# Turning reciprocal row sums on TensorE before their trip through memory, and taking sines two channel blocks at a time

## The chip, the core and the metric

One core of one Trainium2 chip runs the whole program. Its engines work side by side, each in its own order: TensorE (PE; its weight loads are PEld), VectorE (DVE), ScalarE (ACT), GpSimd (POOL) and SyncE (SP), which here issues every transfer between the chip's memory (DRAM) and the on-chip buffers. The metric is the time of one execution on the device in microseconds (us), as a median of runs.

## What is computed

Causal attention over 4 batches, 12 heads, 448 positions and 64 channels per head; a gated block on its result; and a mixing block with sines and cosines. All in float32, 768 channels wide. Cut to what matters:

```
scores = mask(q @ k.T / 8);  attn = exp(scores - max);  attn = attn / (sum(attn) + 1e-9)
x = attn @ v                                   # (batch, 448, 768)
gate = sigmoid(causal_conv5(x, conv_w));  x = (gate * (x @ w_val)) @ w_out
theta = x @ w_theta
y = w_tok_r @ (x * cos(theta)) + w_tok_i @ (x * sin(theta))
u = x + y
out = u + relu(u @ w_ch)
```

## The kernel before

Attention works on pairs of heads, `g` = 0 to 23, six pairs to a batch. `attn_iter(g)` is a generator of ten steps: it transposes the probabilities of pair `g - 1` (`attn_PT`), makes the scores of pair `g` in three portions (`attn_S`: matmuls, then a masked row maximum on DVE at L321, then the exponential with its row sum on ACT at L113), transposes q and k of pair `g + 1` (`attn_T`), and multiplies with v (`attn_AV`, L366).

The division by the row sums is put off: `attn_X1` (L426) multiplies the transposed result by a tile `rb` that holds the reciprocals, one per position, spread over the 64 channels of each head. The reciprocals come out with positions down the partitions (`rec`, 112 partitions by 8), and must be laid along the free axis. In the first batch (`g` < 6) `attn_W` does that with a widened copy and four TensorE transposes. From `g` = 6 on, 18 times, `attn_R` writes `rec` to a DRAM tile `rows` (L389), and `attn_B` reads each head's 448 values back, broadcast over 64 partitions (L415, two transfers). `attn_B` is kept behind the load of the next v.

Everything after the attention is `dense(b)`, a generator as well: six output blocks (`e`) each of x @ w_val, of @ w_out, of the mixing block and of @ w_ch. `gemm` (L496) makes one block: each 128x128 weight block and the activations are split into a high and a low part, and three products of 128x448 are summed, 18 matmuls for six blocks of the inner axis. In the first batch the weights arrive as 64-bit words that DVE and ACT make into floats (`to_f32`, L146 to L153) and POOL and DVE split (L102, L105, L108); the results are stored to DRAM (`plain`, `scratch`) for the later batches, which fetch them (L240, L244).

In the mixing block `theta(e)` copies the angles from the product (L551), reduces them to one turn on DVE (L552, L553), takes the absolute value, and takes a sine (L564) and a cosine (L565) on ACT, each times x (L566 on DVE, L567 on POOL or DVE). The angle tiles `z` rotate over three buffers, which the raw `tok` weights of the first batch use too (`load_tok`). `ztr(e)` transposes both halves on TensorE (L577, seven 128x128 blocks) and splits them (L582 on ACT, L108 on DVE); `tok(e)` (L591) is 21 matmuls with the token weights. Sine and the exponential live in different tables of ACT, so a sine after an exponential is preceded by an ACT_TABLE_LOAD, and the reverse.

A rate table (`RATE`) says after how many steps of `dense(b)` the next step of the attention of batch `b + 1` is written into the program. The order that each engine finally has is then made by a scheduler that replays the written order on a model of the chip: within an engine it may move an instruction ahead of one that waits. `tc.issue_after` pins some instructions: the sines behind the last two exponentials (`PIN`), `attn_B` behind the next v. A PSUM tile of the tags other than "mm" is one of six buffers that rotate.

Of the kernel before, what the change touches and what calls it, by code (L numbers as in the profile page):

```python
# [9 lines left out]
F32 = mybir.dt.float32  # L10
F32R = mybir.dt.float32r
I32 = mybir.dt.int32
# [35 lines left out]
def kernel(  # L48
# [110 lines left out]
    def load_tok(c):  # L159
        t = pool.tile([P, NZ * P], F32, tag=("zt_h", "zt_l")[c % 2], name="tok_raw")  # L160
        for a, w in enumerate((w_tok_r, w_tok_i)):
            r = pool.tile([P, S, 2], I32, tag="z", name="tok_bits", bufs=3)
            nc.sync.dma_start(
                out=r[:CP].rearrange("p n two -> p (n two)"), in_=w[c * CP : (c + 1) * CP, :]
            )
            to_f32(t[:CP, a * S : (a + 1) * S], r[:CP])
# [210 lines left out]
    def attn_R(g):  # L377
# [5 lines left out]
        if g < NP:  # L383
            wide = pool.tile([CP, NC, 2, D], F32, tag="m2k", name="wide", bufs=2)
            nc.vector.tensor_copy(wide, rec.rearrange("p h c -> p c h").unsqueeze(3).broadcast_to((CP, NC, 2, D)))
            wides[g] = wide
            return
        rows = dram.tile([2, NC, CP], F32, tag="rows", name="rows", bufs=2)
        nc.sync.dma_start(out=rows.rearrange("h c p -> p h c"), in_=rec)  # L389
        row_at[g] = rows  # L390
# [125 lines left out]
    def dense(b):  # L516
# [30 lines left out]
        def theta(e):  # L547
            pt = yield from gemm(x2_hl)
            z = pool.tile([P, 2, S], F32, tag="z", name="z", bufs=3)
            t, kk = z[:, 1, :], z[:, 0, :]  # L550
# [7 lines left out]
            else:  # L558
                nc.scalar.activation(kk, t, AF.Abs)
            zri[e] = z  # L560
            with ExitStack() as st:
                for ins in exps[-PIN:]:
                    st.enter_context(tc.issue_after(ins.ins))
                nc.scalar.activation(t, t, AF.Sin, scale=TWO_PI)  # L564
                nc.scalar.activation(kk, kk, AF.Sin, bias=halfpi, scale=-TWO_PI)  # L565
            nc.vector.tensor_tensor(out=kk, in0=kk, in1=x2f[e], op=ALU.mult)  # L566
            (nc.vector if Z_DVE[b] else nc.gpsimd).tensor_tensor(out=t, in0=t, in1=x2f[e], op=ALU.mult)  # L567
            yield

# [32 lines left out]
        yield from theta(1)  # L602
        for e in range(KC):
            if e + 2 < KC:
                g = theta(e + 2)
                next(g)
                yield
                ztr(e)
                yield from g
            elif e + 2 == KC:  # L610
                ztr(e)
                ztr(e + 1)
            yield from tok(e)

        def finish(e):
# [21 lines left out]
    def attn_iter(g):  # L637
# [9 lines left out]
        yield  # L647
        attn_B(h)
        attn_S(g, (2,))
        yield  # L650
        attn_PT(a, (2, 3))
        attn_PT(b, (2, 3))
        yield
        attn_S(g, (3,))
        if h in wides:
# [99 lines left out]
```

## Time and profile before

| | |
|---|---|
| median of 3 runs | 787.95 us (785.98 to 791.84) |
| the profiled execution | 786.97 us |
| its span, first to last instruction | 785.2 us |
| TensorE busy (PE / weight loads) | 727.4 us (93%) / 580.6 us (74%) |
| VectorE, ScalarE, GpSimd busy | 421.5, 403.8, 305.1 us |
| mean granted TensorE clock | 0.966 |
| SP's transfers | 123.86 MB in 148237 packets; 88175 of the program's packets are under 512 bytes |

All figures but the first row come from one profiled execution. An engine's busy time is the union of its instructions. A row of the trace gives the start and the length of an instruction or of a run of them, and in brackets how long its engine sat idle ahead of it and what ended that idle time. [...]

### The profile page before, as it was taken

To read this page: it belongs to the slowest core of one execution; us is meant where nothing else is said; L and a number is where in the kernel's file an instruction comes from. 1 tells how busy PE (TensorE), PEld (TensorE's weight loads), DVE (VectorE), ACT (ScalarE), POOL (GpSimd) and SP (SyncE) were. 2 spreads that over 40 slices of the span, in tenths; PEclk is the share of its full clock that TensorE was granted. 3 is DMA by queue.
4 is the path that set the end of the run, shared out by engine and by line. 5 is a ranking of instruction groups with operands and counts; after the bars stand their busy time and mean duration, and the time that the engine had idled before them with its cause. 6 is when DMAs were issued, how large, how long until landed. Compare 5 with 4: busy or idle time off the path is not lost.

```text
span 785.2 us, 11877 instructions
## 1 busy us (share of the span) xinstructions
PE 727.4 (93%) x3989; PEld 580.6 (74%) x3989; DVE 421.5 (54%) x1026; ACT 403.8 (51%) x975; POOL 305.1 (39%) x331
## 2 busy tenths in 40 slices
PE   6999786878989989999899999999899999999997
PEld 3665655755867777777677887887777788898996
DVE  5887596749646645354546644544547523115531
ACT  5877355648666543645867423434857512125401
POOL 1799725755547473755163400022051141201100
PEclk9999879888989999999999999999999999999999
DMA  9664369688734399989934297786424277774222
GB/s 233 158 192 116 88 193 142 202 181 276 131 117 115 76 225 216 321 228 218 249 85 58 72 202 157 231 205 122 169 73 45 73 184 202 202 218 140 82 73 80
DMA packets 148298, 124.62 MB, mean 159 GB/s; under 512 B 88175, under 2 KB 125837, under 8 KB 148237
## 3 DMA queue, kind: packets, MB, share of 16 engines
q1 hardware_dynamic: 148237, 123.86, 62.7%
q8 instruction: 32, 0.52, 0.3%
q14 instruction: 29, 0.24, 0.1%
HBM read 94.66 MB, written 29.16 MB: 158 GB/s over the span
## 4 chain that ended last, share of the span: by engine, by line
PE 50%; ACT 5%; DMA 4%; DVE 3%; POOL 2%; issue 2%; SPq 0%; ACTq 0%; POOLq 0%
PE ps_mm L496 29%; PE ps_mm L591 9%; PE ps_s L313 3%; PE ps_av L366 3%; PE ps_tr L343 3%; DMA cv_raw<-in_moe_w_ch_dram 2%; PE ps_tr L577 1%; DMA q_raw<-in_q_dram 1%; PE ps_tr L618 1%; ACT L564 1%; ACT prob L113 1%; PE ps_tr L291 1%; DMA scratch<-w_hl 1%; POOL w_hl L105 1%; POOL gate L454 1%
## 5 line engine op out<-in xcount | busy, mean ns | idle before, releaser
L496 PE MATMUL ps_mm<-act_hi,w_hl 128*128 128x448 f32 x864 | 276.6, 384 | 15.8 <-POOL w_hl L105 6.6
L496 PEld LDWEIGHTS ps_mm<-act_hi,w_hl 128*128 128x128 f32 x864 | 165.0, 193 | 45.6 <-issue 10.6
L496 PE MATMUL ps_mm<-act_lo,w_hl 128*128 128x448 f32 x432 | 160.0, 371 | 0.0
L113 ACT ACTIVATE prob<-ps_s,negm 112x112 f32<-112x112 f32 (+1 forms) x192 | 94.8, 500 | 57.6 <-DVE negm L321 34.9
L321 DVE CUSTOM_DVE_ANT_0 ps_s<-ps_s,mask 112x112 f32<-112x112 f32 (+1 forms) x192 | 84.4, 462 | 52.7 <-PE ps_s L313 51.2
L496 PE MATMUL ps_mm<-x_hi,w_hl 128*128 128x448 f32 x264 | 83.9, 388 | 6.2 <-POOL w_hl L102 2.6
L496 PEld LDWEIGHTS ps_mm<-act_lo,w_hl 128*128 128x128 f32 x432 | 83.8, 194 | 5.9 <-issue 0.7
L313 PE MATMUL ps_s<-kt,qt 64*112 64x112 f32 (+3 forms) x384 | 82.0, 447 | 4.0 <-ACT prob L113 2.2
L105 POOL TENSOR_TENSOR act_lo<-x2f,act_hi 128x448 fp32r<-128x448 f32 x36 | 41.7, 1157 | 110.3 <-DVE act_hi L508 72.2
L105 POOL TENSOR_TENSOR w_hl<-cv_raw,w_hl 128x384 fp32r<-128x384 f32 x62 | 64.3, 1039 | 24.1 <-ACT w_hl L224 22.6
L591 PE MATMUL ps_mm<-wtok_h,zt_h 128*128 128x448 f32 x168 | 65.2, 388 | 4.4 <-ACT zt_h L582 4.4
L343 PE MATMUL ps_tr<-ident,prob 112*112 112x112 f32 x480 | 63.0, 265 | 5.9 <-DVE cv_raw L153 4.5
L343 PEld LDWEIGHTS ps_tr<-ident,prob 112*112 112x112 f32 x480 | 50.9, 135 | 19.5 <-DVE cv_raw L153 5.0
L591 PE MATMUL ps_mm<-wtok_h,zt_l 128*128 128x448 f32 x168 | 62.8, 374 | 0.0
L105 POOL TENSOR_TENSOR x_lo<-xf,x_hi 128x448 fp32r<-128x448 f32 x23 | 29.1, 1267 | 86.5 <-ACT x_hi L431 59.0
L496 PEld LDWEIGHTS ps_mm<-x_hi,w_hl 128*128 128x128 f32 x264 | 51.6, 198 | 14.8 <-DVE hf L534 4.2
L591 PE MATMUL ps_mm<-wtok_l,zt_h 128*128 128x448 f32 x168 | 62.1, 370 | 0.0
L567 POOL TENSOR_TENSOR z<-z,x2f 128x448 f32<-128x448 f32 x18 | 20.7, 1153 | 105.2 <-ACT z L564 104.5
L356 ACT COPY pt<-ps_tr 112x448 f32<-112x448 f32 (+3 forms) x132 | 52.2, 431 | 14.0 <-PE ps_tr L343 13.9
L454 POOL TENSOR_TENSOR gate<-gate,tp 128x448 f32<-128x448 f32 x48 | 55.7, 1163 | 1.9
L366 PE MATMUL ps_av<-pt,v_raw 112*64 112x448 f32 (+3 forms) x384 | 55.2, 406 | 0.0
L313 PEld LDWEIGHTS ps_s<-kt,qt 64*112 64x112 f32 x384 | 32.1, 178 | 28.1 <-issue 14.0
(97 smaller groups left out, 1166.3 us busy)
## 6 DMA issues: line engine op xcount, KB each, us to landing
w_hl<-scratch SPq DMA_DIRECT2D x120, 384.0 KB, 4.1
scratch<-w_hl SPq DMA_DIRECT2D x48, 384.0 KB, 4.7
q_raw<-in_q_dram SPq DMA_DIRECT2D x48, 112.0 KB, 3.5
k_raw<-in_k_dram SPq DMA_DIRECT2D x48, 112.0 KB, 3.5
v_raw<-in_v_dram SPq DMA_DIRECT2D x24, 224.0 KB, 8.5
out_dram<-o SPq DMA_DIRECT2D x24, 224.0 KB, 3.5
cv_raw<-in_moe_w_val_dram SPq DMA_DIRECT2D x12, 384.0 KB, 5.0
plain<-cv_raw SPq DMA_DIRECT2D x24, 192.0 KB, 2.9
```

The lines of the kernel that those rows point to most:

```text
L105: nc.gpsimd.tensor_tensor(out=dst, in0=src, in1=f32(hi), op=ALU.subtract)
L113: exps.append(nc.scalar.activation(*args, **kw))
L291: nc.tensor.transpose(pt[:, c * CP : (c + 1) * CP], t[:, c, :, :].rearrange("p h d -> p (h d)"), ident[:CP, :CP])
L313: nc.tensor.matmul(at[j, c], lhsT=qt[j * D : (j + 1) * D, c * CP : (c + 1) * CP], rhs=kt[j * D : (j + 1) * D, :n], start=True, stop=True, ...
L321: ttr = nc.vector.tensor_tensor_reduce(out=at[j, c], in0=at[j, c], in1=mask[:, S - n : S], scale=-1.0 / math.sqrt(D), scalar=3.0e38, op0=A ...
L343: nc.tensor.transpose(pt[:CP, off : off + CP], prob[i, c][:, kc * CP : (kc + 1) * CP], ident[:CP, :CP])
L356: nc.scalar.copy(t, src)
L366: nc.tensor.matmul(av[g][j * D : (j + 1) * D, kc * CP : S], lhsT=tv[:, j, kc, :], rhs=pT.pop((2 * g + j, kc)), start=kc == 0, stop=kc == N ...
L454: nc.gpsimd.tensor_tensor(out=gt, in0=gt, in1=tp, op=ALU.add)
L496: nc.tensor.matmul(pt[:, :S], lhsT=a[:, kc % KH, :], rhs=x, start=kc == 0 and m == 0, stop=kc == KC - 1 and m == 2,)
L567: (nc.vector if Z_DVE[b] else nc.gpsimd).tensor_tensor(out=t, in0=t, in1=x2f[e], op=ALU.mult)
L591: nc.tensor.matmul(pt[:, :S], lhsT=a[:, m, :], rhs=w[:, m, :], start=m == 0 and n == 0, stop=m == NZ - 1 and n == 2,)
```

## The change

1. From `g` = 6 on, `attn_R` transposes `rec` on TensorE (112x8 to 8x112, into a PSUM tile of the six), copies it to a tile `rect` on DVE, and writes `rows` from that: 8 runs of 448 bytes in place of 896 runs of 4 bytes. 18 times each.
2. `attn_B(h)` stands later in `attn_iter`: ahead of the last portion of the scores, no longer ahead of the second.
3. The sines of blocks `e` and `e + 1` are written in one piece, `sines(e)`, at the end of the odd block's `theta`: sine, cosine, sine, cosine, then the four products.
4. The mixing loop is written in pairs: `theta(e + 2)`, `ztr(e)`, `theta(e + 3)`, `ztr(e + 1)`, `tok(e)`, `tok(e + 1)`. Before, the first half of `theta(e + 2)` stood ahead of `ztr(e)`, and `tok(e)` came straight after.
5. The angle tiles have four buffers in place of three.

```diff
     def load_tok(c):
...
-            r = pool.tile([P, S, 2], I32, tag="z", name="tok_bits", bufs=3)
+            r = pool.tile([P, S, 2], I32, tag="z", name="tok_bits", bufs=4)
...
+        pt = psum("tr")
+        nc.tensor.transpose(pt[: 2 * NC, :CP], rec.rearrange("p h c -> p (h c)"), ident[:CP, :CP])
+        rect = pool.tile([2 * NC, CP], F32, tag="rect", name="rect", bufs=1)
+        nc.vector.tensor_copy(rect, pt[: 2 * NC, :CP])
         rows = dram.tile([2, NC, CP], F32, tag="rows", name="rows", bufs=2)
-        nc.sync.dma_start(out=rows.rearrange("h c p -> p h c"), in_=rec)
+        nc.sync.dma_start(out=rows.rearrange("h c p -> (h c) p"), in_=rect)
...
-            z = pool.tile([P, 2, S], F32, tag="z", name="z", bufs=3)
+            z = pool.tile([P, 2, S], F32, tag="z", name="z", bufs=4)
...
             zri[e] = z
+            if e % 2:
+                sines(e - 1)
+            yield
+
+        def sines(e0):
             with ExitStack() as st:
                 for ins in exps[-PIN:]:
                     st.enter_context(tc.issue_after(ins.ins))
-                nc.scalar.activation(t, t, AF.Sin, scale=TWO_PI)
-                nc.scalar.activation(kk, kk, AF.Sin, bias=halfpi, scale=-TWO_PI)
-            nc.vector.tensor_tensor(out=kk, in0=kk, in1=x2f[e], op=ALU.mult)
-            (nc.vector if Z_DVE[b] else nc.gpsimd).tensor_tensor(out=t, in0=t, in1=x2f[e], op=ALU.mult)
-            yield
+                for e in (e0, e0 + 1):
+                    t, kk = zri[e][:, 1, :], zri[e][:, 0, :]
+                    nc.scalar.activation(t, t, AF.Sin, scale=TWO_PI)
+                    nc.scalar.activation(kk, kk, AF.Sin, bias=halfpi, scale=-TWO_PI)
+            for e in (e0, e0 + 1):
+                t, kk = zri[e][:, 1, :], zri[e][:, 0, :]
+                nc.vector.tensor_tensor(out=kk, in0=kk, in1=x2f[e], op=ALU.mult)
+                (nc.vector if Z_DVE[b] else nc.gpsimd).tensor_tensor(out=t, in0=t, in1=x2f[e], op=ALU.mult)
...
-        for e in range(KC):
-            if e + 2 < KC:
-                g = theta(e + 2)
-                next(g)
-                yield
-                ztr(e)
-                yield from g
-            elif e + 2 == KC:
-                ztr(e)
-                ztr(e + 1)
+        for e in range(0, KC - 2, 2):
+            yield from theta(e + 2)
+            ztr(e)
+            yield from theta(e + 3)
+            ztr(e + 1)
             yield from tok(e)
+            yield from tok(e + 1)
+        ztr(KC - 2)
+        ztr(KC - 1)
+        yield from tok(KC - 2)
+        yield from tok(KC - 1)
...
-        attn_B(h)
         attn_S(g, (2,))
         yield
         attn_PT(a, (2, 3))
         attn_PT(b, (2, 3))
         yield
+        attn_B(h)
         attn_S(g, (3,))
```

The program that the scheduler makes of it differs in far more places than these, since a moved step moves its neighbours. Three places matter below.

SP's queue around the trip of pair 8, in the first batch's dense part. Before, the write of `rows` stands ahead of a weight load, and the two reads of `rb` follow three transfers later:

```order
93 L389 DMA rows<-rec 112x8x1
94 L192 DMA cv_raw<-in_moe_w_theta_dram 128x3x256
95 L232 DMA scratch<-w_hl 128x768
96 L280 DMA v_raw<-in_v_dram 112x8x64
97 L415 DMA rb<-rows 64x448 x2
98 L232 DMA scratch<-w_hl 128x768
99 L192 DMA cv_raw<-in_moe_w_theta_dram 128x3x256 x2
```

In the changed program, at the same trip:

```order
93 L192 DMA cv_raw<-in_moe_w_theta_dram 128x3x256 x2
94 L393 DMA rows<-rect 8x112
95 L280 DMA v_raw<-in_v_dram 112x8x64
96 L232 DMA scratch<-w_hl 128x768 x2
97 L192 DMA cv_raw<-in_moe_w_theta_dram 128x3x256
98 L419 DMA rb<-rows 64x448
99 L232 DMA scratch<-w_hl 128x768
100 L419 DMA rb<-rows 64x448
101 L192 DMA cv_raw<-in_moe_w_theta_dram 128x3x256
```

The weight load now goes ahead of the write of `rows`, and the reads of `rb` still stand a few transfers behind it, with loads queued after them.

TensorE at the same pair. Before, the products with v (`ps_av`) stand behind 18 matmuls of a `gemm` that follow the transposes of k, of which the last rows are:

```order
278 L496 MATMUL ps_mm<-act_hi,w_hl 128x448 x2
279 L496 MATMUL ps_mm<-act_lo,w_hl 128x448
280 L496 MATMUL ps_mm<-act_hi,w_hl 128x448 x2
281 L496 MATMUL ps_mm<-act_lo,w_hl 128x448
282 L366 MATMUL ps_av<-pt,v_raw 64x448 x2
```

In the changed program the new transpose (`ps_tr<-ident,rec`) stands there, ahead of the products with v; from the transposes of k to it there are 20 matmuls of a `gemm`, of which the last rows are:

```order
296 L500 MATMUL ps_mm<-act_lo,w_hl 128x448
297 L500 MATMUL ps_mm<-act_hi,w_hl 128x448 x2
298 L500 MATMUL ps_mm<-act_lo,w_hl 128x448
299 L500 MATMUL ps_mm<-act_hi,w_hl 128x448
300 L389 MATMUL ps_tr<-ident,rec 8x112
301 L366 MATMUL ps_av<-pt,v_raw 64x448 x2
```

The products with v stand two matmuls later than before, and behind the transpose of `rec`.

ACT in the mixing block of the second batch. Before, every block's sine and cosine (`z<-z`, and `z<-z,halfpi`) have a table load ahead of them, and the exponentials (`prob`) another:

```order
453 L564 ACT_TABLE_LOAD
454 L564 ACTIVATE z<-z 128x448
455 L565 ACTIVATE z<-z,halfpi 128x448
456 L113 ACT_TABLE_LOAD
457 L113 ACTIVATE prob,sums<-ps_s,negm 112x112
```

In the changed program blocks 4 and 5 have theirs together:

```order
460 L113 ACTIVATE prob,sums<-ps_s,negm 112x448 x2
461 L575 ACT_TABLE_LOAD
462 L575 ACTIVATE z<-z 128x448
463 L576 ACTIVATE z<-z,halfpi 128x448
464 L575 ACTIVATE z<-z 128x448
465 L576 ACTIVATE z<-z,halfpi 128x448
```

Blocks 0 and 1 of the first three batches are still taken one by one there, with exponentials between them. Over the whole program the table loads go from 38 to 26.

## Rows read from the trace of the kernel before

**Rows 1.** Busy time by stretch: length, each engine's busy us, clock, DMA share, GB/s.
```profile
84.00:174.00 90.00, 71.43 (x351) 55.81 (x351) 64.06 (x148) 48.05 (x118) 47.29 (x55) 0.84 0.69 162
174.00:252.00 78.00, 70.71 (x348) 55.41 (x349) 53.37 (x119) 57.60 (x121) 42.66 (x47) 0.88 0.61 163
...
420.00:550.00 130.00, 130.00 (x753) 105.62 (x752) 68.43 (x167) 54.56 (x140) 28.38 (x26) 1.00 0.71 155
...
sum 785.20, PE 727.35 PEld 580.58 DVE 421.47 ACT 403.83 POOL 305.09; mean PE 80.82 PEld 64.51 DVE 46.83 ACT 44.87 POOL 33.90
```
**Rows 2.** TensorE in order of time: idle ahead of an instruction, and what ended it.
```profile
137.67 1.11 PE L496 MATMUL ps_mm<-act_hi,w_hl 128*128 128x448 f32 x2 [5.74 <-POOL w_hl L105]
...
174.14 1.12 PE L496 MATMUL ps_mm<-act_hi,w_hl 128*128 128x448 f32 x2 [5.78 <-ACT act_hi L510]
...
285.62 0.50 PE L343 MATMUL ps_tr<-ident,prob 112*112 112x112 f32 x3 [2.75 <-DVE cv_raw L153]
...
350.29 0.47 PE L496 MATMUL ps_mm<-act_hi,w_hl 128*128 128x448 f32 x1 [1.06 <-ACT w_hl L224]
...
376.50 0.47 PE L496 MATMUL ps_mm<-act_hi,w_hl 128*128 128x448 f32 x1 [1.52 <-DMA w_hl<-scratch]
```
**Rows 3.** The line that writes the reciprocals: count, issue time, time to landing.
```profile
L389 SPq DMA_DIRECT2D rows<-rec x18: 312/431/1304, 77.4 to 628.2; - x18
...
DMA to landing us min/median/max: 6.7/8.2/11.2
```
**Rows 4.** What SP's queue waited for: us in total, times, longest.
```profile
SPq L415 <- DMA rows<-rec: 68.4, 13, 7.5
```
**Rows 5.** Busy time, columns as in the first group, behind one such write (160.71).
```profile
161.00:169.00 8.00, 7.36 (x43) 6.46 (x39) 2.71 (x6) 3.40 (x7) 5.69 (x6) 1.00 0.64 57
```
**Rows 6.** Weight loads, us to landing: those issued in 161 to 169, then all.
```profile
cv_raw<-in_moe_w_theta_dram SPq DMA_DIRECT2D x1, 384.0 KB, 10.9
...
cv_raw<-in_moe_w_theta_dram SPq DMA_DIRECT2D x12, 384.0 KB, 5.5
```
**Rows 7.** The tile that the reciprocals are read back to: time to landing of its transfers.
```profile
DMA to landing us min/median/max: 2.7/3.9/7.3
```
**Rows 8.** Busy time, columns as in the first group, where the clock was low.
```profile
135.00:142.00 7.00, 3.98 (x13) 3.35 (x13) 2.36 (x7) 1.25 (x3) 5.85 (x7) 0.57 0.77 234
...
172.00:179.00 7.00, 4.86 (x16) 4.04 (x18) 4.39 (x10) 4.42 (x9) 4.88 (x6) 0.53 1.07 348
193.00:199.00 6.00, 5.03 (x16) 4.20 (x15) 5.20 (x12) 5.95 (x12) 1.79 (x2) 0.50 0.33 100
```
**Rows 9.** Groups of instructions: table loads, busy us and mean ns.
```profile
L564 ACT ACT_TABLE_LOAD x19 | 24.4, 1283 | 0.3
L113 ACT ACT_TABLE_LOAD x18 | 23.1, 1283 | 0.3
```
**Rows 10.** ACT in order of time, around one table load.
```profile
218.58 1.28 ACT L564 ACT_TABLE_LOAD   x1
219.88 0.58 ACT L564 ACTIVATE z<-z 128x448 f32<-128x448 f32 x1
```
**Rows 11.** TensorE in order of time in the mixing blocks: idle and what ended it.
```profile
190.61 0.98 PE L577 MATMUL ps_tr<-ident,z 128*128 128x128 f32 x7 [2.29 <-DVE z L566]
...
222.91 1.76 PE L577 MATMUL ps_tr<-ident,z 128*128 128x128 f32 x7 [1.93 <-ACT prob L113]
...
564.21 0.74 PE L591 MATMUL ps_mm<-wtok_h,zt_h 128*128 128x448 f32 x1 [1.46 <-ACT zt_h L582]
...
713.38 0.95 PE L577 MATMUL ps_tr<-ident,z 128*128 128x128 f32 x7 [1.22 <-DVE z L566]
```
**Rows 12.** The chain that ended last: start, us, what; one unbroken run of matmuls.
```profile
664.14 21.50 PE ps_mm L496 x106
```
**Rows 13.** Pair 10 in order of time: products with v, and the reciprocal.
```profile
239.02 1.25 PE L366 MATMUL ps_av<-pt,v_raw 112*64 112x448 f32 x6
...
241.53 0.19 DVE L382 RECIPROCAL rec<-rec 112x8 f32<-112x8 f32 x1
```

## The prediction

> **What bounds the kernel now.** I read the busy times by stretch first [rows 1]. TensorE is busy for 727.35 of 785.20 us, and from 420 to 550 us for every microsecond: there no other engine can give anything back. What can be won lies in the 58 us in which TensorE is idle, and in the stretches where its clock was at half. Both cluster in the first batch's dense part: from 84 to 174 us it is busy 71.43 of 90 us at a mean granted clock of 0.84, from 174 to 252 us 70.71 of 78 at 0.88. So the second view is TensorE in order of time, with what ended each idle stretch.
>
> The longest stops are 5.74 and 5.78 us [rows 2]. They end with POOL and ACT, but those had been idle too. Each stop lies some 13 us behind the issue of a write of reciprocals (the second write at 160.71). The third view is that line: 18 writes, which land 6.7 to 11.2 us after issue, median 8.2, for 3.5 KB each [rows 3]. SP, which cannot issue the read of `rb` before that, stood still for 68.4 us in 13 waits with all that is queued behind [rows 4]. And it is more than a wait: from 161 to 169 us the DMA engines are busy for 0.64 of the time and move 57 GB/s [rows 5], where they move 162 on average over 84 to 174 [rows 1]. The one weight load issued in that stretch, right behind the write, landed after 10.9 us, where the median of that line is 5.5 [rows 6]. The 896 runs of 4 bytes lie ahead of it on the same queue. So two things hold the weights: the queue in front of the engines, and the issuer.
>
> **Part A, the trip through memory.** Removed: 888 of 896 runs, 18 times. A write of 8 runs is not in this trace. Its landing is bounded from below by the fastest transfer of the same trip, 2.7 us for the reads back, and from above by their slowest, 7.3 (median 3.9) [rows 7]; I take 3, near the lower end, since the write is 32 times smaller than a read (3.5 against 112 KB). The load behind it then lands in some 5.5 us, 5.4 earlier, and that is nearly all of a 5.78 us stop. Five stops lie behind such a write, with a late load, store or fetch at their root: 5.74, 5.78, 2.75, 1.06 and 1.52, together 16.85 us [rows 2]. Behind the two long ones TensorE went on at half clock: 3.98 us busy at 0.57 and 4.86 us at 0.53 [rows 8], which lost 3.98 x 0.43 + 4.86 x 0.47 = 4.0 us. Upper bound 20.8. Not all of it comes back. DVE is busy 64.06 of the 90 us [rows 1]; without the two stops (11.5) and the slow clock (4.0) the same work would have to fit in 74.5 us, 86% of them, and the next wait for DVE is close. I take 0.6 of the bound, 13 us; the lower bound is half of the two long stops, 6.
>
> `attn_B`, moved later in the text, moves little: SP's queue still has the reads a few transfers behind the write. The pair's result is multiplied by `rb` a whole attention step later, so this I cost at nothing, under the cover of that step (some 30 us per pair in the dense part); without it, DVE would wait one read, 3.9 us.
>
> **Part B, the sines.** Removed are 12 table loads, 4 in each of the first three batches: 19 + 18 become 13 + 12, at 1.283 us each 15.4 us of ACT [rows 9]. ACT has room (57.60 of 78 us even from 174 to 252), so only what TensorE waits for counts. In the mixing blocks I find eleven idle stretches of TensorE that end with ACT, or with what hangs on a sine: four shown, 6.9 us [rows 11], and seven more of 0.61 to 1.41, 5.7 together. Behind three of them the clock was low: one shown, 5.03 us busy at 0.50, lost 2.5 us [rows 8]; the other two 2.7 and 1.3. Upper bound 12.6 + 6.5 = 19.1. The scheduler left blocks 0 and 1 of the first three batches one by one, so the stop of 2.29 us and its slow clock, at block 0 of the first batch, may stay. I take half of what follows in the first batch (idle 3.9 and clock 2.7: 3.3), most of 1.41 in the second and of 0.69 + 1.46 + 1.3 in the third (3, since nine more matmuls of a `gemm` now stand between the first transposes and the first `tok`), and in the last batch 1 of 1.22 + 0.69, since a whole block, 18 x 0.203 = 3.7 us [rows 12], now runs ahead of the first transpose. Together 7. Lower bound 0.
>
> ACT shows a table load at 218.58 with no idle time ahead of it, and the sine 0.02 us after its end [rows 10]: a switch costs the load alone. [...]
>
> **Part C, what it adds.** 18 transposes on TensorE. A matmul in an unbroken run takes 0.203 us for 448 columns [rows 12]; this one has 112, so 3.7 us is the upper bound for 18, and I take 3. 18 copies on DVE, by the reciprocal's 0.19 [rows 13] 3.4 us over the whole run, between work that DVE has slack for; with no slack (first batch, three of them) under 1. An additional PSUM tile of the six per pair is held from the transpose to that copy: free if the copy follows at once; up to the length of the waits below if not.
>
> And a new wait: TensorE now needs `rec`, in order, ahead of the products with v, and those are queued behind it. At pair 10 the products began at 239.02 and the reciprocal ended at 241.72 [rows 13]: had the transpose stood there, TensorE would have waited 2.7 us. Counted so, 12 of the 18 pairs would wait, 15.7 us in all. The scheduler put the transpose later, mostly behind a whole `gemm` block. Bounds 0 and 15.7; I take 4, nearer to the lower end, since outside the first batch and the mixing blocks the reciprocal was ready before the products began, or within a microsecond.
>
> **Sum.** 786.97 (the profiled execution; 1 us under the median of 787.95) - 13 - 7 + 3 + 4 = 774.
>
> **Rivals.** *DVE takes over.* Where the loads come earlier, DVE, at 86%, is late instead: waits keep their place and change their name. A 6, B 2, C 7: 786. For it: DVE's share in the first batch. Against: in the long stops DVE itself was idle.
>
> *The write stays slow.* Its time could be the queue ahead of it, not its runs. Then A is 0, B and C cancel: 787. Against: none of the 18 landed under 6.7 us, while a read 32 times as large does in 2.7.
>
> *Everything comes back.* A 20.8, B 19.1, C 3: 750. Against: the loads of blocks 0 and 1 remain, and DVE's share.
>
> *The transpose holds SP.* The write now waits for TensorE and for DVE's copy, and weight loads queue behind it on SP; TensorE reaches the transpose only through matmuls that need weights. If the block on SP merely moves from behind the write to ahead of it, A is 0 and the full 15.7 + 3.7 are paid: 787 + 19.4 - 7 = 799. It decides once the wait at the transpose is over 1 us on average over the 18 pairs. [...] Against: the queue listing has the weight loads mostly ahead of the write.
>
> **How the numbers follow.** Forecast 0.58 (its own range 764 to 781), everything back 0.10, DVE takes over 0.20, slow write 0.04, transpose holds SP 0.08. About 1% (8 us) is what a measurement of this kernel can tell from no change. Faster: 0.56 of the forecast and the 0.10, 0.66. Same: the rest of the forecast, 0.20 and 0.04, 0.26. Slower 0.08. The range leaves out the lowest half of "everything back" and what lies above the DVE case: 757 to 788.
>
> **What would show it.** A right: the write of `rows` lands in about 3 us, SP's wait for it falls from 68 to under 25 us, no TensorE stop over 3 us from 84 to 174, clock there above 0.92. B right: 25 loads of the two lines, fewer stops that end with ACT from 200 us on. C: idle ahead of the new transpose 4 us in all. I am wrong if the stops of the first batch remain at the same length with DVE or the transpose named, or if the write still lands after 6 us.

## The result

| | before | after |
|---|---|---|
| median | 789.89 us (785.98 to 793.18, 4 runs) | 752.54 us (749.83 to 753.45, 4 runs) |
| ratio to before, 95% interval | | 0.9523 (0.9468 to 0.9579) |
| the profiled execution, its span | 786.97, 785.2 us | 753.18, 751.3 us |
| TensorE busy | 727.4 us | 713.9 us |
| mean granted TensorE clock | 0.966 | 0.982 |

The change is worth 35 us or so, and lies 4.5 us under the range of the prediction (757 to 788, with 774 as the likeliest). TensorE's idle time in the span fell from 57.8 to 37.4 us, 20.4 less; its busy time fell by 13.5, although 18 transposes came in. Most of that is the clock. The granted clock is the share of its full speed that TensorE was given; busy time times the missing share is 727.4 x 0.034 = 24.7 us before and 713.9 x 0.018 = 12.9 after, an estimate from the mean clocks.

The first view of the profile after is TensorE by line: busy us and mean ns, then the idle time just ahead of the line's instructions, and what ended it. The first row is the `gemm`, the second and third are `tok` and `ztr` of the mixing block, the last is the new transpose of the reciprocals:

```profile
L500 PE MATMUL ps_mm<-act_hi,w_hl 128*128 128x448 f32 x864 | 267.2, 374 | 2.4 <-DVE w_hl L108 1.7 <-ACT act_hi L514 0.7
...
L603 PE MATMUL ps_mm<-wtok_h,zt_h 128*128 128x448 f32 x168 | 63.9, 380 | 0.0
...
L589 PE MATMUL ps_tr<-ident,z 128*128 128x128 f32 x168 | 23.5, 282 | 1.6 <-DVE z L579 1.6
...
L389 PE MATMUL ps_tr<-ident,rec 112*8 112x112 f32 x18 | 4.6, 258 | 7.9 <-ACT z L563 4.9 <-DVE rec L382 2.9
```

The kernel before, the same lines:

```profile
L496 PE MATMUL ps_mm<-act_hi,w_hl 128*128 128x448 f32 x864 | 276.6, 384 | 15.8 <-POOL w_hl L105 6.6 <-ACT act_hi L510 6.4 <-DMA w_hl<-scratch 1.5
...
L591 PE MATMUL ps_mm<-wtok_h,zt_h 128*128 128x448 f32 x168 | 65.2, 388 | 4.4 <-ACT zt_h L582 4.4
...
L577 PE MATMUL ps_tr<-ident,z 128*128 128x128 f32 x168 | 24.6, 281 | 6.8 <-DVE z L566 4.2 <-ACT prob L113 1.9 <-DVE xf L426 0.7
```

So two places were cleared. Ahead of the `gemm`, which waited for weights and their splits, 15.8 us became 2.4. In the mixing block 4.4 + 6.8 became 0.0 + 1.6. One place is new, the transposes, with 7.9 us.

By stretch, with the columns of [rows 1] (length, busy us of PE, PEld, DVE, ACT and POOL, clock, DMA share, GB/s):

```profile
84.00:174.00 90.00, 82.91 (x431) 64.49 (x431) 80.77 (x182) 60.80 (x146) 61.55 (x70) 0.94 0.70 206
174.00:252.00 78.00, 74.27 (x425) 59.58 (x426) 56.98 (x131) 53.84 (x125) 47.24 (x52) 0.98 0.51 153
```

In the first batch TensorE is busy for 82.91 of the same 90 us, where it was for 71.43 [rows 1], at a clock of 0.94 for 0.84. DVE did more there as well, 80.77 us, or 90% of the stretch: a share of 86% was not yet a bound.

SP's queue after, what it waited for: in total, times, longest.

```profile
SPq L393 <- DVE rect L391: 15.3, 10, 5.8
SPq L419 <- DMA rows<-rect: 8.1, 10, 3.1
```

The second row answers to [rows 4]: 68.4 us became 8.1. The first is the write waiting for its copy. Before, it waited for the reciprocal in its place, so SP is not held longer there:

```profile
SPq L389 <- DVE rec L382: 18.5, 6, 8.5
```

TensorE in order of time after: what is left of the longer stops, from the start of the dense part on.

```profile
109.20 1.18 PE L343 MATMUL ps_tr<-ident,prob 112*112 112x112 f32 x5 [2.98 <-DVE cv_raw L153]
...
171.64 0.68 PE L500 MATMUL ps_mm<-act_hi,w_hl 128*128 128x448 f32 x2 [1.71 <-DVE w_hl L108]
...
181.25 1.01 PE L291 MATMUL ps_tr<-ident,q_raw 112*128 112x112 f32 x4 [2.66 <-ACT prob L113]
...
360.65 0.26 PE L389 MATMUL ps_tr<-ident,rec 112*8 112x112 f32 x1 [2.67 <-ACT z L563]
...
537.95 0.26 PE L389 MATMUL ps_tr<-ident,rec 112*8 112x112 f32 x1 [2.24 <-ACT z L563]
...
686.17 0.95 PE L589 MATMUL ps_tr<-ident,z 128*128 128x128 f32 x7 [1.61 <-DVE z L579]
```

The stops of 5.74 and 5.78 us [rows 2] have no successor of their size.

### The profile page after: what moved, and what is told of

It is laid out like the page before. It is cut to its first block, busy times and chain, and to the rows that moved or that the text cites. A ratio compares the mean times of both kernels' runs of the same rounds, so it can differ in the third digit from the quotient of the medians.

```text
span 751.3 us, 11926 instructions
## 1 busy us (share of the span) xinstructions
PE 713.9 (95%) x4007; PEld 573.8 (76%) x4007; DVE 432.3 (58%) x1044; ACT 388.3 (52%) x963; POOL 307.6 (41%) x331
## 4 chain that ended last, share of the span: by engine, by line
PE 78%; DVE 10%; ACT 7%; issue 2%; DMA 1%; SPq 1%; POOL 0%; DVEq 0%; ACTq 0%
PE ps_mm L500 38%; PE ps_mm L603 13%; PE ps_s L313 8%; PE ps_av L366 6%; PE ps_tr L343 5%; ACT prob L113 2%; PE ps_tr L589 2%; PE ps_tr L291 2%; DVE ps_cv L146 1%; PE ps_tr L630 1%; DVE ps_cv L149 1%; DVE ps_s L321 1%; PE ps_mm L479 1%; ACT L575 1%; ACT L113 1%
## 5 line engine op out<-in xcount | busy, mean ns | idle before, releaser
L500 PE MATMUL ps_mm<-act_hi,w_hl 128*128 128x448 f32 x864 | 267.2, 374 | 2.4 <-DVE w_hl L108 1.7
L500 PEld LDWEIGHTS ps_mm<-act_hi,w_hl 128*128 128x128 f32 x864 | 161.0, 188 | 30.7 <-issue 15.7
L500 PE MATMUL ps_mm<-act_lo,w_hl 128*128 128x448 f32 x432 | 156.5, 364 | 0.0
L313 PE MATMUL ps_s<-kt,qt 64*112 64x112 f32 (+3 forms) x384 | 83.8, 443 | 5.2 <-ACT prob L113 1.7
L500 PEld LDWEIGHTS ps_mm<-act_lo,w_hl 128*128 128x128 f32 x432 | 81.3, 188 | 5.5 <-issue 0.8
L500 PE MATMUL ps_mm<-x_hi,w_hl 128*128 128x448 f32 x264 | 82.3, 381 | 1.4 <-DVE hf L538 1.0
L105 POOL TENSOR_TENSOR w_hl<-cv_raw,w_hl 128x384 fp32r<-128x384 f32 x62 | 64.5, 1043 | 15.8 <-ACT w_hl L224 14.2
```

The source lines that it names most:

```text
L105: nc.gpsimd.tensor_tensor(out=dst, in0=src, in1=f32(hi), op=ALU.subtract)
L313: nc.tensor.matmul(at[j, c], lhsT=qt[j * D : (j + 1) * D, c * CP : (c + 1) * CP], rhs=kt[j * D : (j + 1) * D, :n], start=True, stop=True, ...
L500: nc.tensor.matmul(pt[:, :S], lhsT=a[:, kc % KH, :], rhs=x, start=kc == 0 and m == 0, stop=kc == KC - 1 and m == 2,)
```

## The experiments

Two questions had to be told apart: which of the five parts of the change gave the time, and by what. The medians of before in these comparisons lie between 785.6 and 787.3 us; each kernel's ratio is to the runs of before beside it. The changed kernel's own ratio, 0.9523, is to a before of 789.89 us. So its distance to another kernel comes out 3 to 6 us larger by ratios than by medians; the text gives the medians' difference, the smaller of the two.

**Part 1 alone.** The reciprocals transposed, everything else as before.

```diff
+        pt = psum("tr")
+        nc.tensor.transpose(pt[: 2 * NC, :CP], rec.rearrange("p h c -> p (h c)"), ident[:CP, :CP])
+        rect = pool.tile([2 * NC, CP], F32, tag="rect", name="rect", bufs=1)
+        nc.vector.tensor_copy(rect, pt[: 2 * NC, :CP])
...
-        nc.sync.dma_start(out=rows.rearrange("h c p -> p h c"), in_=rec)
+        nc.sync.dma_start(out=rows.rearrange("h c p -> (h c) p"), in_=rect)
```

> The kernel before with part 1 of the change alone: the reciprocals transposed on TensorE and written as 8 runs of 448 bytes; attn_B, sines, mixing loop and three angle buffers as before. Theory 'the trip': the write of 896 runs held SP and the DMA queue, and both long stops of the first batch hang on it; five stops (16.9 us) and 4 us of slow clock go, 4 to 8 us are paid at the transpose: 768 to 775, no stop over 3 us from 84 to 174, SP waits under 20 us for rows. Rival 'the sines': the dense part's stops come from ACT and DVE being late, so the trip alone gives less than 8 us: 780 to 788, and stops of like length stay with another name. Rival 'only together': the scheduler's new order is what helps, and neither half gives more than a third of the 34 us.

Measured: 776.71 us, ratio 0.9887 (0.9845 to 0.9929), 9 us faster, and 1.7 us outside the range that the theory of the trip gave. The dense part is repaired as that theory says: no stop of TensorE from 84 to 174 us is over 2.4 us, and SP waits 9.2 us for `rows`. Its stretch, and the same two lines of the mixing block as above:

```profile
84.00:174.00 90.00, 81.21 (x420) 62.75 (x420) 77.21 (x181) 58.19 (x142) 60.28 (x70) 0.94 0.71 205
```

```profile
L595 PE MATMUL ps_mm<-wtok_h,zt_h 128*128 128x448 f32 x168 | 65.7, 391 | 7.8 <-ACT zt_h L586 7.8
...
L581 PE MATMUL ps_tr<-ident,z 128*128 128x128 f32 x168 | 24.1, 279 | 6.3 <-DVE z L570 4.6 <-ACT pt L356 0.9 <-DVE xf L430 0.8
```

From 84 to 174 us nearly all of the change is there already (81.21 busy, clock 0.94). But the stops of the mixing block, 11.2 us before, are now 14.1: part of what the trip gave seems to be lost at the next place.

**Parts 3 to 5 alone.** Sines, loop and buffers as in the change, with the old write and the reads in their old place.

```diff
-            z = pool.tile([P, 2, S], F32, tag="z", name="z", bufs=3)
+            z = pool.tile([P, 2, S], F32, tag="z", name="z", bufs=4)
...
+            if e % 2:
+                sines(e - 1)
...
+        for e in range(0, KC - 2, 2):
+            yield from theta(e + 2)
+            ztr(e)
+            yield from theta(e + 3)
+            ztr(e + 1)
```

> The kernel before with parts 3 to 5 alone: the sines of two blocks together, the mixing loop in pairs, four angle buffers; the write of 896 runs of 4 bytes and the place of attn_B as before. Theory 'the trip': the stops of 5.74 and 5.78 us stay, 8 to 13 us come back, all from the mixing blocks: 775 to 780. Rival 'the sines': 755 to 765, and the long stops of the first batch are gone though the write lands after 7 us or more. 26 table loads in either case.

Measured: 762.99 us, ratio 0.9711 (0.9678 to 0.9744), 23 us faster: the larger part of the change is here, in the range of the rival and not of the theory of the trip. One long stop stays; where the other was, the longest is of 2.07 us, though the write still lands 6.6 to 11.2 us after its issue:

```profile
135.89 1.01 PE L174 MATMUL ps_tr<-ident,tok_raw 112*128 112x112 f32 x4 [5.81 <-DVE cv_raw L153]
...
168.39 0.68 PE L496 MATMUL ps_mm<-act_hi,w_hl 128*128 128x448 f32 x2 [2.07 <-ACT act_hi L510]
```

The same two lines of the mixing block:

```profile
L599 PE MATMUL ps_mm<-wtok_h,zt_h 128*128 128x448 f32 x168 | 64.0, 381 | 2.4 <-ACT zt_h L590 2.2
...
L585 PE MATMUL ps_tr<-ident,z 128*128 128x128 f32 x168 | 22.5, 275 | 1.6 <-DVE z L575 1.6
```

**Part 1 undone in the changed kernel.**

```diff
-        nc.sync.dma_start(out=rows.rearrange("h c p -> (h c) p"), in_=rect)
+        nc.sync.dma_start(out=rows.rearrange("h c p -> p h c"), in_=rec)
```

> The changed kernel with part 1 undone: rec is written from its 112 partitions in 896 runs of 4 bytes, without the transpose and the copy; all else as changed. Theory 'the trip': 770 to 780, stops of 4 to 6 us some 13 us behind the first writes, the write lands after 7 us or more. Rival 'the sines': within 5 us of 752, since the write was only a symptom. The waits ahead of the transpose, 7.9 us in the changed kernel, are gone in either case.

Measured: 763.57 us, ratio 0.9711 (0.9677 to 0.9745), the same as parts 3 to 5 alone. Both forecasts missed: the time lies between their ranges, and the stops of 4 to 6 us did not come back (the longest behind the first two such writes are of 2.68 and 2.30 us), though the write lands after 6.5 us or more. The trip is worth 11 us in the changed kernel, 9 in the one before.

**Part 2 alone.** Only SP's queue changes its order.

```diff
-        attn_B(h)
         attn_S(g, (2,))
...
+        attn_B(h)
         attn_S(g, (3,))
```

> The kernel before with part 2 alone: the reads of rb are issued later; no other engine's order changes, only that of SP's queue. All theories: SP stands still for less than 68 us at the reads, since the write has more time to land ahead of them; if the issuer's standing still is what made the weights late, 5 us or more come back (780 or less); if it is the 896 runs in front of the DMA engines, within 4 us of 788.

Measured: 786.28 us, ratio 1.0005 (0.9973 to 1.0037): nothing. SP's waits at the reads, and the first of the long stops:

```profile
SPq L415 <- DMA rows<-rec: 63.7, 11, 8.5
```

```profile
137.86 1.12 PE L496 MATMUL ps_mm<-act_hi,w_hl 128*128 128x448 f32 x2 [6.28 <-POOL w_hl L105]
```

SP stood for 63.7 us in place of 68.4, so the edit took away too little of the standing to tell whether that or the queue in front of the engines held the weights.

**Parts 3, 4 and 5 one by one, and in pairs.** The edits are those of the diff ahead of the prediction: part 3 with its call of `sines` (old loop, three buffers), part 4 with the new loop and each block's sines left in `theta`, part 5 with the two numbers of buffers.

```diff
-            r = pool.tile([P, S, 2], I32, tag="z", name="tok_bits", bufs=3)
+            r = pool.tile([P, S, 2], I32, tag="z", name="tok_bits", bufs=4)
...
-            z = pool.tile([P, 2, S], F32, tag="z", name="z", bufs=3)
+            z = pool.tile([P, 2, S], F32, tag="z", name="z", bufs=4)
```

Part 3 alone:

> The kernel before with part 3 alone: the sines of two blocks in one piece; the mixing loop in its old order, three angle buffers, old write. 26 table loads in place of 38. Theory 'table loads': the 23 us of parts 3 to 5 come from the switches of ACT's table, and are all here: 762 to 768. Rival 'buffers': the sines alone give the 7 us that the prediction counted, 776 to 782, and the fourth buffer the rest, since the raw token weights of the first batch rotate over the same buffers. Rival 'loop': 776 or more, and the pairs of the loop the rest.

Part 4 alone:

> The kernel before with part 4 alone: the mixing loop in pairs, each block's sine and cosine by themselves, three angle buffers, old write. Theory 'table loads' and rival 'buffers': within 5 us of 786. Rival 'loop': 770 to 776, since the transposes of an angle block get a whole gemm more of time behind its sine.

Part 5 alone:

> The kernel before with part 5 alone: four buffers in place of three for the angles and the raw token weights. Theory 'table loads' and rival 'loop': within 5 us of 786. Rival 'buffers': 768 to 776, with shorter stops from 84 to 174 us, where the token weights arrive.

Parts 3 and 4:

> The kernel before with parts 3 and 4: sines of two blocks together and the loop in pairs, but three angle buffers, old write. Parts 4 and 5 alone gave 12.4 and 3.2 us, part 3 alone nothing, and all three 23. Theory 'sines need the loop': the pair of sines comes later than a single one and pays only where the transposes are moved back as well: 763 to 767, and the fourth buffer is worth little. Rival 'buffers': 770 to 774 as with the loop alone, and the rest comes with the fourth buffer. Rival 'parts add up': 773.

Parts 4 and 5:

> The kernel before with parts 4 and 5: the loop in pairs and four buffers, every block's sines by themselves (32 table loads), old write. Theory 'sines need the loop': 768 to 773. Rival 'buffers': 762 to 766, as with all three, so that the sines are worth nothing in any company. Rival 'parts add up': 770.

Parts 3 and 5:

> The kernel before with parts 3 and 5: sines of two blocks together and four buffers; old loop, old write. Theory 'sines need the loop': 780 to 788, as with the buffers alone or worse. Rival 'the buffers free the sines': 772 to 778.

The changed kernel without part 3:

> The changed kernel with part 3 undone: every block's sine and cosine by themselves behind its angles; loop in pairs, four buffers, new write. Theory 'sines need the loop': 758 to 765. Rival 'buffers': within 4 us of 752, since the loop and the buffers gave all. Rival 'parts add up': within 4 us of 752 too.

The changed kernel without part 4:

> The changed kernel with part 4 undone: the mixing loop in its old order, with tok straight behind ztr; sines of two blocks together, four buffers, new write. Theory 'sines need the loop': the loop's 12 us are lost and the sines' 8 with them, 770 to 776, with stops ahead of tok and ztr in all four mixing blocks. Rival 'parts add up': 762 to 766. Rival 'the trip covers it': under 758.

The changed kernel without part 5:

> The changed kernel with part 5 undone: three buffers for the angles and the raw token weights. Alone the fourth buffer gave 3 us, beside the sines and the loop 8. If it works by letting the first batch's weights in earlier, which the new write does as well: 753 to 757, and 84 to 174 us no worse than before this edit. If it works by letting the pair of sines run ahead: 759 to 764, with the loss in the mixing blocks, from 165 us on.

Measured, as medians in us (ratio to before in brackets):

| | sines singly, 3 buffers | sines in pairs, 3 | singly, 4 | in pairs, 4 |
|---|---|---|---|---|
| old loop, old write | before | 787.92 (1.0024) | 782.45 (0.9963) | 781.96 (0.9936) |
| new loop, old write | 773.16 (0.9846) | 770.81 (0.9804) | 770.33 (0.9785) | 762.99 (0.9711) |
| old loop, new write | 776.71 (0.9887) | - | - | 770.11 (0.9809) |
| new loop, new write | - | 755.15 (0.9595) | 761.12 (0.9689) | 752.54 (0.9523) |

The intervals reach some 0.003 to 0.006 to either side. Each of these edits makes the scheduler lay out the whole program anew, so a difference of 2 or 3 us between two kernels may be the order's and not the edit's. The forecasts of "loop", and from the pairs of parts on those of "sines need the loop", hold in these runs with one exception: for parts 3 and 4 with three buffers the rival "buffers" came true, so the sines in pairs seem to need the fourth buffer as well. The last row and "old loop, new write" in the last column have the reads moved as well, which alone is worth nothing.

The loop decides. It gives 12 to 19 us with the old write, down each column, and 17.6 with the new one. The sines in pairs give nothing under the old loop, neither alone nor with four buffers, though they take away 12 table loads; beside the new loop and four buffers they give 7.3 and 8.6, beside the new loop with three 2.4, which is not told apart from nothing. The fourth buffer gives 3 us alone, 8 beside loop and sines, and 2.6 in the changed kernel, where the intervals of the two ratios overlap (0.9557 to 0.9633 without it). That the new write leaves it so little is what the forecast of 753 to 757 said: it works by letting the first batch's weights in earlier, and the new write does as well. The traces bear that out. The second of the long stops, of 5.78 us at 174.14 in the kernel before [rows 2], stays with the old write and three buffers (4.16 to 6.18 us in the three such kernels of the table with an edit); in all five kernels with the old write and four buffers no stop there is over 2.6 us. Part 4 alone, and part 5 alone, where the first long stop stays:

```profile
173.05 1.12 PE L496 MATMUL ps_mm<-act_hi,w_hl 128*128 128x448 f32 x2 [6.18 <-ACT act_hi L510]
```

```profile
136.27 1.01 PE L174 MATMUL ps_tr<-ident,tok_raw 112*128 112x112 f32 x4 [6.38 <-DVE cv_raw L153]
...
165.08 0.47 PE L496 MATMUL ps_mm<-act_hi,w_hl 128*128 128x448 f32 x1 [1.87 <-POOL w_hl L102]
```

With part 5 alone SP issues the last load of raw token weights at 101.0 us, in the kernel before at 111.2.

What the loop does is seen in the lines of `tok` and `ztr`. The kernel with part 3 alone, that with part 4 alone, and the changed kernel without part 4, each with the idle time ahead of `tok` and of `ztr`:

```profile
L599 PE MATMUL ps_mm<-wtok_h,zt_h 128*128 128x448 f32 x168 | 64.6, 385 | 4.7 <-ACT zt_h L590 3.1 <-DMA q_raw<-in_q_dram 1.5
...
L585 PE MATMUL ps_tr<-ident,z 128*128 128x128 f32 x168 | 23.7, 278 | 7.7 <-DVE z L575 4.7 <-DVE xf L426 1.5 <-ACT prob L113 1.5
```

```profile
L591 PE MATMUL ps_mm<-wtok_h,zt_h 128*128 128x448 f32 x168 | 63.9, 380 | 2.0 <-ACT zt_h L582 1.9
...
L577 PE MATMUL ps_tr<-ident,z 128*128 128x128 f32 x168 | 22.1, 274 | 0.3 <-DVE zt_l L108 0.2
```

```profile
L603 PE MATMUL ps_mm<-wtok_h,zt_h 128*128 128x448 f32 x168 | 65.0, 387 | 6.3 <-ACT zt_h L594 6.3
...
L589 PE MATMUL ps_tr<-ident,z 128*128 128x128 f32 x168 | 24.5, 283 | 9.9 <-DVE z L579 8.5 <-DVE xf L430 1.4
```

12.4, 2.3 and 16.2 us. With the old order TensorE waits for the product of a sine, transposes, and waits again for ACT's split of those transposes. In the written order the old loop has half a `gemm`, 9 matmuls, in each of these two gaps; the new one has a whole one, 18. A pair of sines is written one block later for the even block, and the old loop does not move the transposes back with it. The third pair of rows fits that: where the weights come in time and the sines come in pairs, but the loop is old, the mixing block costs 16.2 us of stops, 5 more than in the kernel before, and in all four batches. That the longer gaps are the cause is read from the written order and these rows; no kernel changed a gap alone.

**The runs of 4 bytes by themselves.** The changed kernel with a second, useless write of the reciprocals behind the useful one.

```diff
         nc.sync.dma_start(out=rows.rearrange("h c p -> (h c) p"), in_=rect)
+        junk = dram.tile([2, NC, CP], F32, tag="junk", name="junk", bufs=2)
+        nc.sync.dma_start(out=junk.rearrange("h c p -> p h c"), in_=rec)
```

> The changed kernel with, behind each write of rows from rect, a second write of the same reciprocals as 896 runs of 4 bytes to a DRAM tile that nobody reads: the cost of the runs by itself, since nothing waits for them but what is queued behind them. Theory 'queue': the runs delay the loads queued behind them, and most of what part 1 gave is lost again: 760 to 768. Rival 'issuer': it was SP's standing still for the landing that cost, and here it does not stand: within 4 us of 752.

Measured: 770.16 us, ratio 0.9815 (0.9761 to 0.987). 17.6 us came back, about 1 us for each of the 18 writes. That is outside what "queue" expected, on its side; but SP did stand again, in which the expectation was wrong:

```profile
SPq L421 <- DMA rows<-rect: 57.4, 13, 6.8
```

The scheduler put the useless write ahead of the useful one (in the first batch's dense part at 156.48 and 161.25 us), and SP waited up to 6.8 us for the small write behind it on the same queue, 3.1 at most in the changed kernel. SP also stood for the reciprocals at the useless write:

```profile
SPq L395 <- DVE rec L382: 21.1, 9, 5.0
```

So what such a write costs in this kernel is shown, with all that it brings; how it divides between loads held in the queue, SP standing still and the new order of the program is not, and stays open. A useless second write of 8 runs, which would take the runs by themselves, was not tried, nor a write on another queue.

**The wait ahead of the new transposes.** Both kernels are the changed one with the transpose, the copy and the write behind the products with v: for all 18 pairs, and from pair 12 on.

```diff
+        rec_at[g] = rec
+        if g < 2 * NP:      # only in the second kernel
+            attn_R2(g)
...
         attn_AV(h)
+        attn_R2(g)
         load_v(g + 1)
```

> The changed kernel, but with the transpose of the reciprocals, its copy and the write of rows written behind the products with v in place of ahead of them. If the 7.9 us that TensorE waits ahead of the transposes, with the slow clock behind two of them, are lost time: 744 to 750, idle there under 2 us. If the wait only stands in for one that comes anyway, or the later write now makes rb late: 751 to 758.

> The changed kernel; the transpose of the reciprocals written behind the products with v from pair 12 on, ahead of them as in the change for pairs 6 to 11. With all 18 moved, the stretch behind the tenth pair was 5 us shorter than in the changed kernel, and the one ahead of it as much longer. If the wait ahead of the transposes is real time wherever TensorE is the bound: 746 to 750. If the order of the first batch decides and the rest follows it: 750 to 756.

Measured: 753.56 us (0.958, 0.9532 to 0.9628) and 749.01 us (0.9531, 0.9493 to 0.9568), neither told apart from the changed kernel, though the second lies in the range of the forecast that called the wait real time. With all moved, the idle time ahead of the transposes is gone, but part of it stands at the products with v in its place. The second row is the successor of the stop of 2.67 us at 360.65:

```profile
L397 PE MATMUL ps_tr<-ident,rec 112*8 112x112 f32 x18 | 4.7, 259 | 0.0
```

```profile
363.65 0.60 PE L366 MATMUL ps_av<-pt,v_raw 112*64 112x448 f32 x2 [1.52 <-ACT prob L113]
```

Both hang on ACT's exponentials of the same portion. The row of 360.65 names another instruction of ACT, which the transpose does not read; what it reads is the reciprocal, which ended at 360.51. In the changed kernel ACT, in order of time around that stop, has its table load at 357.43 ahead of the exponentials, and DVE the reciprocal behind them:

```profile
357.43 1.28 ACT L113 ACT_TABLE_LOAD   x1
358.73 0.64 ACT L113 ACTIVATE prob<-ps_s,negm 112x448 f32<-112x448 f32 x1
...
359.35 0.63 ACT L113 ACTIVATE prob<-ps_s,negm 112x448 f32<-112x448 f32 x1
...
360.31 0.20 DVE L382 RECIPROCAL rec<-rec 112x8 f32<-112x8 f32 x1
```

The transpose needs the reciprocals of sums that both exponentials make. The products with v start behind the first of them, whose result they do not read; that they wait for the PSUM buffer it frees is likely and not shown. A stop of 2.67 us became one of 1.52, and over the whole kernel no gain that these runs can tell was left of the 7.9 us; 749.01 is the lowest median of all kernels here, but its ratio is that of the changed kernel.

**No trip at all.** The changed kernel with the first batch's way for all 24 pairs.

```diff
-        if g < NP:
+        if True:
             wide = pool.tile([CP, NC, 2, D], F32, tag="m2k", name="wide", bufs=2)
```

> The changed kernel without any trip through memory: all 24 pairs spread their reciprocals as the first six do, by a widened copy on DVE and four TensorE transposes. 54 more transposes than in the change, 14 us at the 0.26 us that each of its own takes, and 18 writes and 36 reads fewer. If the transfers still cost in the changed kernel: 752 or less; if the transposes are all that is left to pay: 758 to 766.

Measured: 755.55 us, ratio 0.9599 (0.9556 to 0.9642). TensorE is busy for 718.4 us, 4.5 more; 18 writes and 36 reads fewer do not pay for it. The time lies between the two forecasts, and its interval overlaps that of the changed kernel: what the transfers still cost there is about what the added transposes and widened copies cost, or less. With the 54 transposes TensorE's busy time rose by these 4.5 us, from 713.9, and not by the 14 that the expectation counted.

**Part 2 undone in the changed kernel.** The reads of `rb` in their old place.

```diff
+        attn_B(h)
         attn_S(g, (2,))
...
-        attn_B(h)
         attn_S(g, (3,))
```

> The changed kernel with part 2 undone: the reads of rb written ahead of the second portion of the scores, as before. With the old write the move was worth nothing. If it stays so: within 4 us of 752. If SP now stands at the reads while the copy and the write are late: 756 to 762, with over 25 us of SP's waits there in place of 8.

Measured: 754.12 us, ratio 0.9584 (0.9542 to 0.9626); SP waits 8.4 us at the reads, as against 8.1. The move is worth nothing with either write.

## Why the prediction was wrong

The step that failed is part B of the sum. It stood at 7 us, with 19.1 as its upper bound; parts 3 to 5 gave 23 without part 1, and 24 with it (776.71 to 752.54). Three things in that step were wrong.

*The cause of the stops.* The prediction's list holds the right stops for the mixing blocks: the idle time ahead of `ztr` and `tok` went from 11.2 to 1.6 us. But the step put them down to the sines' table loads and then halved them because blocks 0 and 1 kept theirs. The runs show that the edit that takes the loads away does not clear them: 12 fewer under the old loop changed nothing (787.92), the new loop with 4 of them gone gave 12 us. The loop stood in the prediction as half a sentence ("nine more matmuls of a `gemm` now stand between the first transposes and the first `tok`"), priced together with the sines at 3 us in the second and third batches, and as "a whole block" at 1 in the last.

*The bound was not a bound.* Its list ended at the mixing blocks, with 12.6 us idle and 6.5 lost to the slow clock. In the kernel with parts 3 to 5 alone, beside the one before, TensorE's idle time fell by 10.3 us (57.8 to 47.5), and its busy time, for the same 3989 matmuls, by 14.2 (727.4 to 713.2), in one execution of each. By the mean clocks, 0.966 and 0.982, some 12 of the 14.2 are slow clock (727.4 x 0.034 less 713.2 x 0.018, an estimate). So the slow clock was mis-sized in B, 6.5 for some 12, and part of the idle time that came back stood elsewhere: the second long stop, 5.78 us, which the prediction gave to the trip and not to B, came down to 2.07 with the old write in place.

*The fourth buffer had no price at all.* It gave 3 us alone and 8 beside the loop and the sines, and that second long stop is under 2 us with it alone. From 84 to 174 us TensorE is then busy for 76.58 us, where it was for 71.43 [rows 1], with the old write still in place:

```profile
84.00:174.00 90.00, 76.58 (x373) 59.55 (x373) 67.05 (x153) 51.35 (x124) 51.64 (x60) 0.85 0.71 178
```

So one of the five stops of part A was not the write's alone: the new write clears it, and the fourth buffer does too. In the changed kernel, where both are in place, the buffer is worth 2.6 us, with overlapping intervals.

Parts A and C, taken together, were nearly right. The forecast for the trip less its price was 13 - 7 = 6 us; measured were 9 alone and 11 in the changed kernel. With B's 23 the 9 make 32, where both together gave 35; that is too little to say that the two repairs are worth more together. The signs that the prediction asked for are there: SP's wait for the write at 8.1 us (under 25 was forecast), no stop over 3 us from 84 to 174, clock there 0.94 (over 0.92), the two lines with 13 + 12 table loads. The size of A was held down by DVE's 86%; the profile after shows that DVE still let 11.5 us more of TensorE's work into the same 90 us. How long the new write takes to land is not in the trace; SP, which stands behind it, waited at most 3.1 us, which fits the 3 us taken.

C was too small: the idle time ahead of the transposes is 7.9 us, not 4, and the 18 transposes are busy for 4.6 us, not 3, over the 3.7 that was taken as their upper bound. The stop at 360.65 was followed by TensorE at a granted clock of 0.50 from 362 to 365 us, and of 0.66 on average over this stretch of the profile after:

```profile
361.00:366.00 5.00, 5.00 (x27) 3.31 (x26) 3.78 (x7) 3.67 (x7) 1.14 (x1) 0.66 0.01 3
```

Of that no gain was left that the kernels with the late transpose can tell.

The copy behind the transpose did make DVE wait: it stood 13.7 us ahead of five of the 18 copies until TensorE had made the transpose. The view of that line of the kernel after, us and times:

```profile
  PE ps_tr L389: 13.7, 5
```

That work which was ready stood behind these copies is not shown: behind each of the five DVE's next instruction, the product with `rb`, started only after another 1.78 to 2.23 us of idle time. The rival of the transpose that holds SP did not come true: it was to decide once the wait at the transpose is over 1 us on average, and 7.9 us over 18 pairs are 0.44.

The rival that came nearest was "everything comes back", at 750, with a chance of 0.10. What spoke against it, the loads left at blocks 0 and 1 and DVE's share, did not hold. Its number came near and its terms did not: B gave more than its 19.1, A and C together less than its 17.8. The range was cut at the middle of that case, and so missed.

## What to carry to other kernels

When a diff moves work on the engine that is the bound, price the new distance between producer and consumer by itself. Here two waits in a row each end with another engine (sine to transpose, transpose to split to matmul), and a loop that puts more independent matmuls into each gap cleared most of them with the sines left as they were (11.2 us of stops became 2.3); the sines in pairs paid 7 to 9 us only beside that loop and the fourth buffer. And a list of stops in the blocks that a diff touches is no upper bound for what the diff gives: here a buffer shared with another stage cleared a stop outside the list (5.78 us became 1.87), and more slow clock went than the list had (some 12 us for 6.5, an estimate from the mean clocks).

A stop can have more than one remedy. Before it is put down to one cause, ask which other part of the diff brings its work forward; a kernel with that part alone tells.

Ask into how many runs a small write is cut when its queue carries bulk loads. Here the same 3.5 KB in 8 runs in place of 896, with the transposes that this took, gave 9 to 11 us over 18 writes, and a useless extra write of 896 runs, with the waits that it brought, cost about 1 us of the whole kernel each time.

## What the runs showed of the hardware

Twelve ACT_TABLE_LOADs, 15.4 us of ACT at 1.283 us each, went without any gain where the loop stayed as it was (787.92 us against 785.60, ratio 1.0024, 0.9998 to 1.0051). The same edit also moves the sines, so what the loads by themselves are worth is not shown. ACT is busy for 403.8 of 785.2 us and has room for them; at 357.43 us above, one stands ahead of exponentials that TensorE waits for.

The write of 3.5 KB in 896 runs took 6.7 to 11.2 us to land [rows 3], and as a useless extra write it went with SP standing 57.4 us in place of 8.1 for a write of 8 runs behind it on the queue.
